# Column parts for the scale weights, five V banks for batch 0, and a new text order in a DiT attention block on one core

## The chip, the cores and the metric

The kernel runs on one core of one Trainium2 chip. The metric is device microseconds of one execution (lower is better), as the median of several runs. The four runs of the kernel before lie 0.3% apart (120.02 to 120.33 us). "Ratio" means throughout: the mean time of one kernel's fast runs over the mean time of the kernel before's fast runs of the same rounds, so it is not quite the ratio of the medians that are quoted beside it. Two runs of experiments were marked slow (over 1.5% above the fastest of their kernel); they are named, and no ratio uses them. The medians in the tables are of all runs.

TensorE is the matmul engine, VectorE and ScalarE do elementwise work, and the DMA engines bring weights from memory. The weight loads are issued in program order by SyncE's queue.

## The reference, cut to what matters

Two streams, image (2 x 256 tokens) and text (2 x 32 tokens), with D = 1152, bf16. Both are layer-normed and modulated by columns of `silu(c) @ wmod` (shift, scale, gate), projected to q, k, v, attend to each other jointly, and are projected out behind the gate.

```python
mod_i = (_silu(c) @ wmod_img).reshape(B, 6, 1, D)   # shift, scale, gate are used
mod_t = (_silu(c) @ wmod_txt).reshape(B, 6, 1, D)
hi = _layernorm(x_img) * (1 + sci) + shi ; ht = _layernorm(x_txt) * (1 + sct) + sht
qkvi = hi @ wqkv_img ; qkvt = ht @ wqkv_txt
# q, k, v = text and image tokens one behind the other
p = softmax(q k^T * D**-0.5) ; a = p v
out_i = x_img + gai * (ai @ wo_img) ; out_t = x_txt + gat * (at @ wo_txt)
```

There are 14 weight matrices of 1152 x 1152 (2.65 MB each), 37 MB in all, and they are read once.

## The kernel before

The kernel keeps five weights at a time in SBUF, the on-chip memory. Each weight goes into one of five slots, and a load into a slot can't be issued before the last reader of that slot's previous weight is done. As all loads stand in one queue, a load that waits also holds up those behind it: in the trace of the change the text gate's load is issued at 80.78 us, and the next one, for the image output weights, starts at 82.42 us.

```python
def load_w(slot, src, c0, splits=(D,)):      # columns c0.. of src into slot "w<slot>"
    ...
w_sc_i = wtile(0)                            # image scale
w_v_i = wtile(1)                             # image V
for b in range(B):
    nc.sync.dma_start(x_i[:, b * TPB:(b + 1) * TPB, :], ...)
SCC = (0, 4, 7, K8, KT)
for r0, r1 in zip(SCC, SCC[1:]):             # scale by groups of 128 rows, whole rows of 2304 bytes
    nc.sync.dma_start(w_sc_i[:, r0:r1, :], sc_v[:, r0:r1, :])
for r0, r1 in ((0, 1), (1, 2), (2, 3), (3, 5), (5, 7), (7, KT)):
    nc.sync.dma_start(w_v_i[:, r0:r1, :], v_v[:, r0:r1, :])
w_sh_i = load_w(2, wmod_img, 0)
w_q_i = load_w(3, wqkv_img, 0)
w_sh_t = load_rows(0, wmod_txt, 0)           # load_rows: three DMAs of three row groups each
w_k_i = load_w(4, wqkv_img, D)
w_sc_t = load_w(1, wmod_txt, D)
w_q_t = load_w(2, wqkv_txt, 0)
w_k_t = load_w(3, wqkv_txt, D)
w_v_t = load_w(1, wqkv_txt, 2 * D)
w_ga_i = load_w(0, wmod_img, 2 * D)          # image gate
w_ga_t = load_w(2, wmod_txt, 2 * D)          # text gate, in the slot of text q
w_o_i = load_rows(3, wo_img, 0)
w_o_t = load_rows(1, wo_txt, 0)
```

At the start the scale columns are computed by TensorE (`sc_ps`), transposed by VectorE, and multiplied into the normalised and transposed x. The V matmuls follow, then image q and k with text work between the blocks, and then:

```python
# in image k, before its last block: qk_txt(0, w_q_t)
qk_txt(1, w_k_t)
...
scores_txt()
scores_img(0)
img_gate()        # 36 matmuls with w_ga_i; then a 0.59 MB broadcast DMA of the result (tile gb)
scores_img(1)
v_txt()
p_transposes(0)
txt_gate()        # 36 matmuls with w_ga_t, row groups 0 to 8 in order
attn_pair(G[0], G[1])
...               # rest of attention, then the output projection
```

All TensorE instructions are pinned to program order, so a wait at `txt_gate` stops everything behind it (in the change TensorE runs nothing from 88.8 to 92.5 us).

## Time and profile before

| | before |
|---|---|
| median of 4 runs | 120.25 us (120.02 to 120.33) |
| span of the profiled run | 118.6 us |
| TensorE busy | 112.1 us, 95% |
| first V matmul / image q starts | 14.76 / 35.03 us |
| text gate's rows start / first output matmul | 87.18 / 95.43 us |
| text gate weight: issued, landed | 73.06 us, 85.7 us |

The chain of work that ended last, in order of time (start, length, what):

```profile
2.12 9.85 DMA t<-in_wmod_img_dram
...
13.83 0.49 DVE scc L217
...
14.76 2.12 PE vps L61 x9
...
87.18 1.22 PE gps L61 x36
88.39 2.16 PE aps L61 x18
...
95.43 19.52 PE ps L61 x144
```

At the start the chain is the scale weights' DMA, then their matmuls, the transpose and the first V matmul. From 14.76 us on it is TensorE alone. Two sets of windows follow, at the start and before the text gate. A row has the window in us, its length, the busy time of TensorE, its weight loads, VectorE, ScalarE and GpSimd, each with the number of instructions, and then the granted clock, the DMA engines' busy share and their GB/s:

```profile
4.00:6.00 2.00, 2.00 (x9) 0.72 (x8) 1.57 (x5) 1.33 (x4) 0.59 (x5) 1.00 0.99 392
6.00:8.00 2.00, 2.00 (x11) 0.81 (x9) 1.02 (x4) 1.94 (x7) 0.46 (x4) 1.00 1.02 393
```

```profile
78.00:80.00 2.00, 2.00 (x22) 1.54 (x17) 1.26 (x3) 0.81 (x2) 0.00 (x0) 1.00 1.04 406
80.00:82.00 2.00, 2.00 (x44) 1.32 (x43) 1.68 (x8) 0.96 (x5) 0.00 (x0) 1.00 1.03 410
```

The line of SyncE's queue that issues the text gate weight (start, time spent, what):

```profile
73.06 0.37 SPq L89 DMA_DIRECT2D t<-in_wmod_txt_dram  x1
```

This DMA landed 12.6 us after its issue, at 85.7 us, because the queue still held other bytes in front of it (at 409 GB/s some 5.2 MB moved in that time, and this weight is 2.65 MB of them). It was wanted at 87.18 us, so the slack is 1.5 us.

### The profile page before, as it was taken

The page shows a single profiled execution, that of the slowest core. Times are in us where ns is not written, and L with a number is a line of the kernel's source. Part 1 is how long each engine was busy: PE and PEld are TensorE (multiplying, and loading weights), DVE is VectorE, ACT ScalarE, POOL GpSimd, SP SyncE. Part 2 cuts the span into 40 slices and gives each one's busy share as a digit, 9 for nine tenths or more (in the row PEclk, how much of TensorE's full clock was granted, in tenths as well). Part 3 has the DMA queues.
Part 4 walks back from the last instruction along what each step waited for, and adds up shares of the span by engine and source line. Part 5 has one row for each costly group of instructions (what it writes and reads, how often), then busy time and mean ns, then how long its engine had stood idle before and what let it go on. Part 6 is the DMA issues. An engine that isn't in the chain of part 4 may idle for free.

```text
span 118.6 us, 2515 instructions
## 1 busy us (share of the span) xinstructions
PE 112.1 (95%) x1051; PEld 64.0 (54%) x1059; DVE 75.3 (63%) x157; ACT 41.8 (35%) x86; POOL 10.3 (9%) x31
## 2 busy tenths in 40 slices
PE   4988899999999999999999999999999999999990
PEld 1335544445674444445444457877876666666660
DVE  2568592063966799999999540048685666666571
ACT  4799620041752524323039233345327620000000
POOL 7110000000000000000000000000409017000000
PEclk9999999999999999999999999999999999999998
DMA  4999999999999999999999999999999996220223
GB/s 104 382 392 399 404 410 406 413 412 411 411 389 384 413 412 410 405 413 411 412 413 412 410 407 413 412 404 412 405 408 411 412 389 219 109 89 16 99 50 100
DMA packets 18613, 40.86 MB, mean 345 GB/s; under 512 B 1019, under 2 KB 1547, under 8 KB 18603
## 3 DMA queue, kind: packets, MB, share of 16 engines
q1 hardware_dynamic: 17728, 39.56, 85.7%
q0 software_dynamic: 480, 0.89, 2.2%
q10 hardware_dynamic: 395, 0.26, 0.7%
q8 instruction: 8, 0.13, 0.4%
q14 instruction: 2, 0.02, 0.0%
HBM read 39.38 MB, written 1.34 MB: 343 GB/s over the span
## 4 chain that ended last, share of the span: by engine, by line
PE 86%; DMA 8%; DVE 2%; SPq 1%; issue 1%; DVEq 0%
PE ps L61 52%; PE vps L61 15%; DMA t<-in_wmod_img_dram 8%; PE gps L61 6%; PE aps L61 6%; PE sps L61 5%; PE sc_ps L61 1%; PE pT_ps L64 1%; SPq L104 1%; DVE tmp L629 1%; DVE o L630 0%; DVE scc L217 0%; SPq L108 0%; PE tpt L64 0%; PE tp L64 0%
## 5 line engine op out<-in xcount | busy, mean ns | idle before, releaser
L61 PE MATMUL ps<-xT_i,t 128*128 128x512 bf16 x157 | 35.6, 380 | 0.3
L61 PEld LDWEIGHTS <-t 128*128 128x128 bf16 x324 | 20.4, 98 | 19.2 <-issue 0.7
L395 DVE SCALAR_TENSOR_TENSOR acc_sh<-t,sTf,acc_sh 128x1152 f32<-128x1152 bf16 x16 | 21.3, 1404 | 0.0
L61 PE MATMUL ps<-t,aT 128*128 128x384 bf16 (+3 forms) x153 | 20.2, 308 | 0.0
L61 PE MATMUL vps<-t,hS_i 128*128 128x512 bf16 (+1 forms) x106 | 17.8, 325 | 0.3 <-DVE hS_i L248 0.2
L61 PEld LDWEIGHTS <-aT 128*128 128x128 bf16 (+1 forms) x153 | 13.0, 101 | 7.1 <-issue 0.5
L61 PEld LDWEIGHTS <-hS_i 128*128 128x128 bf16 x108 | 9.0, 98 | 8.8 <-DVE hS_i L248 0.3
L629 DVE TENSOR_TENSOR tmp<-ps,gb 128x384 bf16<-128x384 f32 (+2 forms) x13 | 6.8, 526 | 6.3 <-PE ps L61 6.3
L346 ACT ACTIVATE qkT<-ps 128x512 bf16<-128x512 f32 (+2 forms) x11 | 6.2, 561 | 12.1 <-PE ps L61 12.1
L61 PE MATMUL wps<-warm 128*128 128x512 bf16 x25 | 7.7, 458 | 1.6 <-DVE unit L132 1.5
L481 POOL DMA_DIRECT2D mod_scratch<-g_sb x4 | 2.5, 634 | 76.6 <-ACT g_sb L174 76.6
L348 ACT CAST qkT<-ps 128x512 bf16<-128x512 f32 (+2 forms) x11 | 5.9, 554 | 8.3 <-PE ps L61 8.3
L172 DVE CAST v_i<-vps 128x512 bf16<-128x512 f32 x5 | 3.5, 692 | 8.2 <-PE vps L61 8.2
L553 DVE TENSOR_TENSOR half<-sps,half 64x288 f32<-64x288 f32 x1 | 0.4, 448 | 9.0 <-ACT half L552 9.0
L587 DVE TENSOR_SCALAR aT<-aps,svc 128x288 bf16<-128x288 f32 x9 | 4.5, 518 | 2.6 <-PE aps L61 2.5
L61 PEld LDWEIGHTS <-sT 128*32 128x32 bf16 x180 | 4.5, 96 | 2.8 <-issue 2.2
L174 ACT CAST v_i<-vps 128x512 bf16<-128x512 f32 x4 | 2.3, 580 | 10.0 <-PE vps L61 10.0
L61 PE MATMUL sps<-qkT 128*128 128x288 bf16 (+1 forms) x54 | 5.6, 288 | 0.0
L61 PEld LDWEIGHTS <-warm 128*128 128x128 bf16 x26 | 2.6, 111 | 5.2 <-issue 2.1
L61 PE MATMUL aps<-pT,v_i 128*128 128x288 bf16 x36 | 5.3, 288 | 0.0
L589 ACT ACTIVATE aT<-aps,svc 128x288 bf16<-128x288 f32 x9 | 4.1, 498 | 3.0 <-PE aps L61 2.9
L61 PE MATMUL gps<-t,sT 128*32 128x288 bf16 x144 | 5.1, 287 | 0.0
(104 smaller groups left out, 108.0 us busy)
## 6 DMA issues: line engine op xcount, KB each, us to landing
t<-in_wqkv_txt_dram SPq DMA_DIRECT2D x3, 2592.0 KB, 16.5
t<-in_wmod_img_dram SPq DMA_DIRECT2D x2, 2592.0 KB, 13.9
t<-in_wqkv_img_dram SPq DMA_DIRECT2D x2, 2592.0 KB, 20.1
t<-in_wmod_txt_dram SPq DMA_DIRECT2D x2, 2592.0 KB, 15.5
t<-in_wmod_txt_dram SPq DMA_DIRECT2D x3, 864.0 KB, 14.7
t<-in_wo_img_dram SPq DMA_DIRECT2D x3, 864.0 KB, 12.3
t<-in_wo_txt_dram SPq DMA_DIRECT2D x3, 864.0 KB, 11.4
t<-in_wqkv_img_dram SPq DMA_DIRECT2D x3, 576.0 KB, 9.2
```

Of the source, the lines that this page charges most:

```text
L61: return pin(nc.tensor.matmul(*a, **k))
L64: return pin(nc.tensor.transpose(*a, **k))
L104: nc.sync.dma_start(x_i[:, b * TPB:(b + 1) * TPB, :], x_img[b].rearrange("(p t) d -> p t d", t=TPB))
L172: nc.vector.tensor_copy(out_ap, in_ap)
L174: nc.scalar.copy(out_ap, in_ap)
L346: nc.scalar.mul(out_ap, in_ap, SCALE)
L348: nc.scalar.copy(out_ap, in_ap)
L395: pin(eng.scalar_tensor_tensor(acc[:, b, :], w[:, kt, :], sTf[:, kt, b:b + 1], acc[:, b, :], op0=ALU.mult, op1=ALU.add))
L481: nc.gpsimd.dma_start(gsc[si, b, :].rearrange("(g j) -> g j", g=NGG), g_sb[b:P:32, :])
L587: nc.vector.tensor_scalar(dst, tiles[(b, dt)][:], bias, None, op0=ALU.add)
L589: nc.scalar.activation(dst, tiles[(b, dt)][:], ACT.Identity, bias=bias)
L629: nc.vector.tensor_mul(tmp[:, 0:n], ps[:, 0:n], gb[:, b, c0:c0 + n])
```

## The change

The early part tries to start V sooner. The scale weights are loaded and used in two column parts (512 and 640 columns, so rows of 1024 and 1280 bytes), x of batch 1 is loaded behind part one and V row 0, and V of batch 0 runs over its first four row groups in five PSUM banks while part two is still on its way. The load of image q is cut into two column parts too. The late part moves text q behind the image gate, loads the image gate ahead of text V, and loads both gates by rows. Cut to its core (`...` marks cuts; the evacuation, transpose and V helpers that serve the early part are left out):

```diff
-    for b in range(B):
+    def load_x(b):
         nc.sync.dma_start(x_i[:, b * TPB:(b + 1) * TPB, :], ...)
...
+    KA = 4
+    SCP = ((0, KA), (KA, KT))
+    load_x(0)
+    load_sc(0, ((0, 4), (4, K8), (K8, KT)))       # 512 columns
+    load_v(((0, 1),))
+    load_x(1)
+    load_v(((1, 2), (2, 3), (3, KA)))
+    load_sc(1, ((0, 5), (5, K8), (K8, KT)))       # 640 columns
+    load_v(((KA, 5), (5, 7), (7, KT)))
...
-    w_q_i = load_w(3, wqkv_img, 0)
+    w_q_i = load_w(3, wqkv_img, 0, (5 * P, D - 5 * P))
...
     w_k_t = load_w(3, wqkv_txt, D)
+    w_ga_i = load_rows(0, wmod_img, 2 * D)
     w_v_t = load_w(1, wqkv_txt, 2 * D)
-    w_ga_i = load_w(0, wmod_img, 2 * D)
-    w_ga_t = load_w(2, wmod_txt, 2 * D)
+    w_ga_t = load_rows(2, wmod_txt, 2 * D)
...
-    A0 = [(0, 0), (1, 0), (0, 1), (1, 1)]
+    A0 = [(0, 0), (1, 0), (0, 1), (1, 1), (0, 2)]
...
-    qk_img(w_k_i, 1, {1: (txt_shift_split, txt_rows_scale,),
-                      6: (txt_rows_shift, txt_cols_shift, txt_modulate),
-                      8: (lambda: qk_txt(0, w_q_t),)})
+    qk_img(w_k_i, 1, {1: (txt_transposes, txt_shift_split), 3: (txt_rows_scale,),
+                      7: (txt_rows_shift, txt_cols_shift, txt_modulate)})
...
-    scores_txt()
     scores_img(0)
     img_gate()
+    qk_txt(0, w_q_t)
+    scores_txt()
     scores_img(1)
```

More of the change, by code (lines that the diff above doesn't have):

```diff
@@ L55, with tr_tile @@
     ps_mm = ctx.enter_context(tc.tile_pool(name="ps_mm", bufs=6, space=PSUM))
-    ps_tr = ctx.enter_context(tc.tile_pool(name="ps_tr", bufs=2, space=PSUM))
+    ps_tr = ctx.enter_context(tc.tile_pool(name="ps_tr", bufs=1, space=PSUM))
+    tr_turn = [0]
+    def tr_tile(shape, dtype, which=None, name="tr"):
+        if which is None:
+            which = tr_turn[0] % 2
+            tr_turn[0] += 1
+        return ps_tr.tile(shape, dtype, tag="tr%d" % which, name=name)
     pin = tc.keep_in_program_order
@@ L102, with load_sc, load_v @@
     sc_v, v_v = wview(wmod_img, D), wview(wqkv_img, 2 * D)
-    for b in range(B):
+    def load_x(b):
         nc.sync.dma_start(x_i[:, b * TPB:(b + 1) * TPB, :], x_img[b].rearrange("(p t) d -> p t d", t=TPB))
-    SCC = (0, 4, 7, K8, KT)
-    for r0, r1 in zip(SCC, SCC[1:]):
-        nc.sync.dma_start(w_sc_i[:, r0:r1, :], sc_v[:, r0:r1, :])
-    for r0, r1 in ((0, 1), (1, 2), (2, 3), (3, 5), (5, 7), (7, KT)):
-        nc.sync.dma_start(w_v_i[:, r0:r1, :], v_v[:, r0:r1, :])
+    KA = 4
+    SCP = ((0, KA), (KA, KT))
+    def load_sc(part, rows):
+        c0, c1 = SCP[part][0] * P, SCP[part][1] * P
+        for r0, r1 in rows:
+            nc.sync.dma_start(w_sc_i[:, r0:r1, c0:c1], sc_v[:, r0:r1, c0:c1])
+    def load_v(rows):
+        for r0, r1 in rows:
+            nc.sync.dma_start(w_v_i[:, r0:r1, :], v_v[:, r0:r1, :])
+    load_x(0)
[5 more added lines that the diff above has]
+    load_v(((KA, 5), (5, 7), (7, KT)))
     w_sh_i = load_w(2, wmod_img, 0)
-    w_q_i = load_w(3, wqkv_img, 0)
+    w_q_i = load_w(3, wqkv_img, 0, (5 * P, D - 5 * P))
     w_sh_t = load_rows(0, wmod_txt, 0)
@@ L157 @@
     pin(nc.vector.tensor_mul(s18[:], c18[:], e18[:]))
-    sT_ps = ps_tr.tile([P, B * KT], bf, tag="tr")
+    sT_ps = tr_tile([P, B * KT], bf)
     tr(sT_ps[:], s18[:], ident[0:B * KT, 0:B * KT])
     sT = const.tile([P, KT, B], bf)
-    warm_up(14)
+    warm_up(10)
     def silu_cols():
@@ L175, in evac, with ln_stats @@
         evac_idx[0] += 1
-    def ln_stats(x_ap, np_, between=None):
+    def ln_stats(x_ap, np_, between=None, at=1):
         stats = small.tile([P, NCH, 6], f32, tag="stats")
         for k in range(NCH):
-            if k == 1 and between:
+            if k == at and between:
                 between()
@@ L185, in ln_stats, with ln_sum @@
         return mv
-    def ln_sums(x_ap, junk):
-        sm = small.tile([P, 3], f32, tag="lnact")
-        pin(nc.scalar.activation(junk, x_ap, ACT.Copy, scale=1.0 / D, accum_out=sm[:, 0:1]))
-        pin(nc.scalar.activation(junk, x_ap, ACT.Square, scale=float(D) ** -0.5, accum_out=sm[:, 1:2]))
-        return sm
+    def ln_sum(x_ap, junk, sm, col):
+        if col == 0:
+            pin(nc.scalar.activation(junk, x_ap, ACT.Copy, scale=1.0 / D, accum_out=sm[:, 0:1]))
+        else:
+            pin(nc.scalar.activation(junk, x_ap, ACT.Square, scale=float(D) ** -0.5, accum_out=sm[:, 1:2]))
     def ln_var(sm):
@@ L218, in mod_cols_of, with sc_rows @@
         return t
-    sc_ps = ps_mm.tile([P, KT, LW], f32, tag="mm")
-    def sc_rows(r0, r1):
+    sc_ps = [ps_mm.tile([P, KA, LW], f32, tag="mm", name="sc_a"), None]
+    sc1_i = const.tile([P, KT, LW], f32, name="scc", tag="scc")
+    def sc_rows(part, r0, r1):
+        c0, c1 = SCP[part]
+        ps = sc_ps[part]
         if r0 == 0:
             for g in range(NGG):
-                mm(sc_ps[LW * g:LW * g + LW].rearrange("p c l -> p (c l)"), lhsT=unit[:], rhs=warm[:, 0:KT * LW],
-                   start=True, stop=False, tile_position=(0, LW * g))
+                mm(ps[LW * g:LW * g + LW].rearrange("p c l -> p (c l)"), lhsT=unit[:],
+                   rhs=warm[:, 0:(c1 - c0) * LW], start=True, stop=False, tile_position=(0, LW * g))
@@ L227, in sc_rows @@
         for kt in range(r0, r1):
             for g in range(NGG):
-                mm(sc_ps[LW * g:LW * g + LW], lhsT=sT32[:, kt, :], rhs=group(w_sc_i, kt, g),
+                mm(ps[LW * g:LW * g + LW], lhsT=sT32[:, kt, :], rhs=group(w_sc_i, kt, g)[:, c0:c1],
                    start=False, stop=(kt == KT - 1), tile_position=(0, LW * g))
-    def x_transposes(k0, b):
-        tr_pool = b == 1 or k0 < 6
-        tp = (ps_tr if tr_pool else ps_mm).tile([P, 3, NI], bf, tag="tr" if tr_pool else "mm", name="tp")
-        for kt in range(k0, k0 + 3):
-            for t in range(TPB):
-                i = b * TPB + t
-                tr(tp[:, kt - k0, t * P:(t + 1) * P], xn_i[:, i, kt * P:(kt + 1) * P], ident[:])
-        dst = xT_i[:, k0:k0 + 3, b * NI:(b + 1) * NI]
-        def copy_out():
-            pin(nc.vector.tensor_copy(dst, tp[:]) if k0 == 3 else nc.scalar.copy(dst, tp[:]))
-        return copy_out
@@ L246, in x_scale, with sc_cols, x_transposes @@
-    def x_scale(k0, k1, b):
+    def sc_cols(part):
+        c0, c1 = SCP[part]
+        pin(nc.vector.transpose(sc1_i[:, c0:c1, :].rearrange("p c l -> p (c l)"),
+                                sc_ps[part][:].rearrange("p c l -> p (c l)")))
+    def x_transposes(k0, k1, tiles, which):
+        n = len(tiles)
+        tp = tr_tile([P, k1 - k0, n * P], bf, which, name="tp")
+        for kt in range(k0, k1):
+            for t, i in enumerate(tiles):
+                tr(tp[:, kt - k0, t * P:(t + 1) * P], xn_i[:, i, kt * P:(kt + 1) * P], ident[:])
+        return lambda op: pin(op(xT_i[:, k0:k1, tiles[0] * P:(tiles[0] + n) * P], tp[:]))
@@ L247, in x_scale @@
+    def x_scale(k0, k1, tiles):
+        b, c0, c1 = tiles[0] // TPB, tiles[0] * P, (tiles[-1] + 1) * P
         for kt in range(k0, k1):
-            pin(nc.vector.tensor_scalar(hS_i[:, kt, b * NI:(b + 1) * NI], xT_i[:, kt, b * NI:(b + 1) * NI],
-                                        sc1_i[:, kt, b:b + 1], None, op0=ALU.mult))
+            pin(nc.vector.tensor_scalar(hS_i[:, kt, c0:c1], xT_i[:, kt, c0:c1], sc1_i[:, kt, b:b + 1], None,
+                                        op0=ALU.mult))
     VW = 512
@@ L253, with v_mm, v_rows, v_keys @@
     accs = {}
-    def v_open(ids, k0, k1, kt_major=True):
-        for key in ids:
-            if key not in accs:
-                accs[key] = ps_mm.tile([P, VW], f32, tag="mm", name="vps")
-        loop = [(kt, key) for kt in range(k0, k1) for key in ids] if kt_major else \
-            [(kt, key) for key in ids for kt in range(k0, k1)]
-        for kt, (i, cc) in loop:
-            mm(accs[(i, cc)][:], lhsT=hS_i[:, kt, i * P:(i + 1) * P], rhs=w_v_i[:, kt, cc * VW:(cc + 1) * VW],
-               start=(kt == 0), stop=(kt == KT - 1), skip_group_check=True)
-            if kt == KT - 1:
-                evac(v_i[:, i, cc * VW:(cc + 1) * VW], accs[(i, cc)][:])
-    A0 = [(0, 0), (1, 0), (0, 1), (1, 1)]
-    A1 = [(2, 0), (3, 0)]
+    def v_mm(kt, key):
+        i, cc = key
+        if key not in accs:
+            accs[key] = ps_mm.tile([P, VW] if cc < 2 else [P, TPB, P], f32, tag="mm", name="vps")
+        acc = accs[key]
+        if cc < 2:
+            mm(acc[:], lhsT=hS_i[:, kt, i * P:(i + 1) * P], rhs=w_v_i[:, kt, cc * VW:(cc + 1) * VW],
+               start=(kt == 0), stop=(kt == KT - 1), skip_group_check=True)
+        else:
+            for t in range(TPB):
+                mm(acc[:, t, :], lhsT=hS_i[:, kt, (i + t) * P:(i + t + 1) * P], rhs=w_v_i[:, kt, 2 * VW:D],
+                   start=(kt == 0 and t == 0), stop=(kt == KT - 1), skip_group_check=True)
+        if kt == KT - 1:
+            if cc < 2:
+                evac(v_i[:, i, cc * VW:(cc + 1) * VW], acc[:])
+            else:
+                evac(v_i[:, i:i + TPB, 2 * VW:D], acc[:])
+    def v_rows(ids, k0, k1):
+        for kt in range(k0, k1):
+            for key in ids:
+                v_mm(kt, key)
+    def v_keys(ids, k0, k1):
+        for key in ids:
+            for kt in range(k0, k1):
+                v_mm(kt, key)
+    A0 = [(0, 0), (1, 0), (0, 1), (1, 1), (0, 2)]
     def ln_norm_dve(i, mv):
@@ L274, in ln_norm_act @@
         ln_norm(x_i[:, i, :], sm[:, 0:1], ln_rstd(sm[:, 2:3], P, sign=-1.0), P, xn_i[:, i, :])
-    s0 = ln_sums(x_i[:, 0, :], xn_i[:, 0, :])
+    V, A = nc.vector.tensor_copy, nc.scalar.copy
+    T0, T2, T3 = (0, 1), (2,), (3,)
+    sm0, sm3 = [small.tile([P, 3], f32, tag="lnact", name="sm") for _ in range(2)]
+    for col in range(2):
+        ln_sum(x_i[:, 0, :], xn_i[:, 0, :], sm0, col)
     m1 = ln_stats(x_i[:, 1, :], P, between=silu_cols)
-    ln_var(s0)
+    ln_var(sm0)
     ln_norm_dve(1, m1)
-    ln_norm_act(0, s0)
@@ L281 @@
-    s2 = ln_sums(x_i[:, 2, :], xn_i[:, 2, :])
-    m3 = ln_stats(x_i[:, 3, :], P)
-    ln_var(s2)
-    r3, r2 = ln_rstd(m3[:, 1:2], P), ln_rstd(s2[:, 2:3], P, sign=-1.0)
-    ln_norm(x_i[:, 3, :], m3[:, 0:1], r3, P, xn_i[:, 3, :])
-    ln_norm(x_i[:, 2, :], s2[:, 0:1], r2, P, xn_i[:, 2, :])
-    for out in [x_transposes(k0, 0) for k0 in (0, 3, 6)]:
-        out()
-    sc_rows(0, 4)
-    warm_up(3)
-    sc_rows(4, 7)
-    warm_up(1)
-    out01 = x_transposes(0, 1)
-    sc_rows(7, K8)
-    sc_rows(K8, KT)
@@ L296 @@
-    out31 = x_transposes(3, 1)
-    sc1_i = mod_cols_of(sc_ps, "scc")
-    out01()
-    x_scale(0, 3, 0)
-    out61 = x_transposes(6, 1)
-    v_open(A0, 0, 3)
-    out31()
-    out61()
-    for k0 in (0, 3, 6):
-        for b in range(B):
-            if k0 or b:
-                x_scale(k0, k0 + 3, b)
-    v_open(A1, 0, 3)
-    v_open(A0 + A1, 3, KT - 2)
-    v_open(A0 + A1, KT - 2, KT, kt_major=False)
+    ln_norm_act(0, sm0)
+    sc_rows(0, 0, 4)
+    warm_up(2)
+    sc_rows(0, 4, K8)
+    out_a = x_transposes(0, 2, T0, 0)
@@ new lines @@
+    sc_rows(0, K8, KT)
+    out_b = x_transposes(2, 5, T0, 1)
+    out_a(A)
+    sc_cols(0)
+    x_scale(0, 2, T0)
+    out_b(V)
+    x_scale(2, KA, T0)
+    v_rows(A0, 0, 1)
+    out_c = x_transposes(5, KT, T0, 0)
+    v_rows(A0, 1, KA)
+    m2 = ln_stats(x_i[:, 2, :], P)
+    for col in range(2):
+        ln_sum(x_i[:, 3, :], xn_i[:, 3, :], sm3, col)
+    ln_norm_dve(2, m2)
+    out_c(A)
+    ln_var(sm3)
+    out_a = x_transposes(0, KA, T2, 1)
+    out_a(A)
+    sc_ps[1] = tr_tile([P, KT - KA, LW], f32, 0, name="sc_b")
@@ new lines @@
+    sc_rows(1, 0, 5)
+    x_scale(0, KA, T2)
+    ln_norm_act(3, sm3)
+    out_b = x_transposes(KA, KT, T2, 1)
+    out_b(A)
+    v_rows([(2, 0)], 0, KA)
+    sc_rows(1, 5, K8)
+    sc_rows(1, K8, KT)
+    sc_cols(1)
+    out_a = x_transposes(0, K8, T3, 1)
+    for kt in range(KA, KT):
+        x_scale(kt, kt + 1, T0)
+        x_scale(kt, kt + 1, T2)
+    out_a(A)
+    v_rows(A0 + [(2, 0)], KA, KA + 1)
+    out_b = x_transposes(K8, KT, T3, 0)
+    out_b(A)
+    v_rows(A0 + [(2, 0)], KA + 1, KT - 2)
@@ L312, in mod_rows_of @@
+    x_scale(0, KT, T3)
+    v_keys(A0 + [(2, 0)], KT - 2, KT)
+    v_keys([(3, 0)], 0, KT)
     def mod_rows_of(w, lhs):
-        gps = ps_tr.tile([P, KT, LW], f32, tag="tr")
+        gps = tr_tile([P, KT, LW], f32)
         for kt in range(KT):
@@ L318, in mod_rows_of @@
         return gps
-    v_open([(2, 1)], 0, KT)
+    v_keys([(2, 1)], 0, KT)
     p_sh = mod_rows_of(w_sh_i, sT32)
@@ L333 @@
     pin(nc.scalar.dma_start(x_t[:], xt_flat[:, :]))
-    v_open([(3, 1)], 0, KT)
-    def v_last():
-        vps = ps_mm.tile([P, NIT, P], f32, tag="mm")
-        for i in range(NIT):
-            for kt in range(KT):
-                mm(vps[:, i, :], lhsT=hS_i[:, kt, i * P:(i + 1) * P], rhs=w_v_i[:, kt, 2 * VW:D],
-                   start=(kt == 0), stop=(kt == KT - 1))
-        evac(v_i[:, :, 2 * VW:D], vps[:])
+    v_keys([(3, 1), (2, 2)], 0, KT)
     def qk_evac(out_ap, in_ap, blk):
@@ L383, in txt_transposes @@
     def txt_transposes():
-        tpt = ps_tr.tile([P, KT, NTT], bf, tag="tr")
+        tpt = tr_tile([P, KT, NTT], bf)
         for kt in range(KT):
@@ L423, in txt_rows_shift @@
     def txt_rows_shift():
-        gps = ps_tr.tile([P, KT, LW], f32, tag="tr")
+        gps = tr_tile([P, KT, LW], f32)
         rows["sh"] = vec_rows(halves[acc_sh.name], gps,
@@ L500, in txt_gate @@
                                     gsc[1, b, :].rearrange("(r g j) -> g r j", r=2, g=2)[g].partition_broadcast(NT))
-    v_last()
     shift_v_rows()
-    qk_img(w_q_i, 0, {1: (txt_ln,), 2: (txt_shift_part(0, 3),), 5: (txt_shift_part(3, 6),),
-                      6: (txt_transposes,), 8: (txt_shift_part(6, KT),)})
-    qk_img(w_k_i, 1, {1: (txt_shift_split, txt_rows_scale,),
-                      6: (txt_rows_shift, txt_cols_shift, txt_modulate),
-                      8: (lambda: qk_txt(0, w_q_t),)})
+    qk_img(w_q_i, 0, {1: (txt_shift_part(0, 3),), 3: (txt_ln,), 4: (txt_shift_part(3, 6),),
+                      7: (txt_shift_part(6, KT),)})
+    qk_img(w_k_i, 1, {1: (txt_transposes, txt_shift_split), 3: (txt_rows_scale,),
+                      7: (txt_rows_shift, txt_cols_shift, txt_modulate)})
     qk_txt(1, w_k_t)
@@ L558, in p_transposes @@
     def p_transposes(b):
-        pT_ps = ps_tr.tile([P, 3, NTOK], bf, tag="tr")
+        pT_ps = tr_tile([P, 3, NTOK], bf)
         for qi in range(TPB):
```

## The prediction

> **What bounds the kernel now.** The chain of waits is TensorE for 86%, and DMA only at the start. The timeline shows TensorE without a gap from the first V matmul (14.76 us) to the last output matmul (about 115 us): the windows give 99.9 us busy in those 100.2 us. Until 14.76 it waits for the scale weights: x (1.18 MB) and scale (2.65 MB) must land (first four rows at 9.85 us, next three at 12.0, the last about 13), then a 0.48 us column transpose and a 0.28 us scaling. The DMA engines are almost as tight: 405 to 413 GB/s, busy share 1.04, from 4 us to 95 us. Each 2.65 MB weight costs 6.5 us of it, and weights land about 1.5 us after the transferred bytes reach their place in the order.
>
> **What the change does at the start.** Part one needs only 0.59 MB of x and 1.18 MB of scale, landing at about 8.5 us (my estimate from the landing curve); the layernorm of batch 0 already ended at 8.8 us. So V of batch 0 can start near 10 us. Rows 0 to 3 in five banks cost 4 x (4 x 0.216 + 2 x 0.056) = 3.9 us, and tile 2 another 0.86 us, all in time that was warm-up. Then TensorE waits again: scale part two is byte 5.0 MB and V row 4 byte 5.3 MB of the order, so the second scaling comes at about 17.4 us (17 to 18). From there V is dense. Sum: 4.8 us done early, 2.6 us later dense start: gain about 2.1 us (1.5 to 2.7) when q starts (35.0 becomes about 32.9). [...]
>
> **What happens to that gain.** The bytes are unchanged, so the text gate weight stays at byte 33.0 MB; it landed at 73.06 + 12.6 = 85.7 us and was needed at 87.18: slack 1.5 us. TensorE 2.1 us earlier meets that. Worse, it lies in the slot of text q. Text q moves behind the image gate, so the slot comes free at about 78.5 us instead of 73.06, when the bytes before it (30.4 MB) have passed at about 78: the queue runs dry for about 1.3 us. Worse again, the image gate comes 5 us earlier, so its broadcast (0.59 MB, 1.4 us of bandwidth, which today runs at 89 to 96 us) now shares the engines with the text gate weight. Estimated landing 87 to 88.5 us against 85 us wanted: TensorE waits 1.5 to 3 us before the text gate's rows (loading by rows hides only the first two thirds), and attention starts at 87 to 88.8 us against 88.4 now. After it all is TensorE work as before (26.6 us).
>
> So most of the early gain is given back. Floor: without stall the text gate still can't end before 86.1 us, a gain of 2.3 us.
>
> **Predicted:** 119.7 us, 118.3 to 121.0. Faster by over 2%: 9%; within 2%: 85%; slower: 6%.
>
> **To check:** first V matmul near 10 us; TensorE gap near 15 to 17.5 us ending on scale or V weights; q starting at 32.3 to 33.5; a DMA wait of over 1 us at the text gate's rows; a dip in GB/s near 78 to 80 us; attention to end unchanged.
>
> **What would make it wrong:** the text shift's VectorE sums (22.9 us) end later and stop the key blocks; scale part two lands later than the curve says; the broadcast does not collide or the queue does not run dry (then 118.2).

The sum of the early gain: 3.9 + 0.86 = 4.76 us done early, less 17.4 - 14.76 = 2.64 us of later dense start, is 2.12 us, about 2.1. With about 1.5 us lost at the text gate, 120.25 - 2.1 + 1.5 comes to the 119.7 us.

For its other terms the traces show: 90 matmuls of 128x512 in 19.53 us (0.217 us each, the chain of the change from 34.92 us on), and in the trace of before six of 128x128 in 0.33 us (0.055 each), 407 GB/s on average from 4 to 95 us with slices down to 382, and 33.07 MB through the weight queue by 84.2 us, 1.5 us before the text gate weight landed.

## More of the kernel before

Lines of the profile's page. The rows cut the span into 40 slices of 2.97 us; a digit is the busy share in tenths, PEclk is the granted TensorE clock in tenths, GB/s is what the DMA engines moved.

```profile
PE   4988899999999999999999999999999999999990
...
PEclk9999999999999999999999999999999999999998
...
GB/s 104 382 392 399 404 410 406 413 412 411 411 389 384 413 412 410 405 413 411 412 413 412 410 407 413 412 404 412 405 408 411 412 389 219 109 89 16 99 50 100
```

TensorE is full from the sixth slice on, at full clock, and the DMA engines are full too: 382 to 413 GB/s in slices 2 to 33, over 400 in 26 of these 32.

## The result, and the profile after

| | before | after |
|---|---|---|
| median | 120.25 us (4 runs) | 126.53 us (126.27 to 127.74, 4 runs) |
| ratio of fast runs | | 1.0545, 95% interval 1.0475 to 1.0616 |
| span of the profiled run | 118.6 us | 125.8 us |
| mean granted clock, profiled run | 0.995 | 0.973 (the other three runs: 0.986, 0.969, 0.986) |
| first V matmul / dense V stretch | 14.76 / 14.76 us | 10.62 / 19.37 us |
| image q starts | 35.03 us | 34.92 us |
| text gate's rows start | 87.18 us | 87.02 us |
| first output matmul | 95.43 us | 102.59 us |

The change is slower, well outside the stated range. The profiled run of the change was the slowest of its four (127.74 us), so the sums below are somewhat larger than those of the median. The same lines of the page (slices of 3.15 us here):

```profile
PE   5998979999999999999999999998159999999990
...
PEclk9999999999999999999999999999955899999999
...
GB/s 130 295 363 402 397 403 412 413 397 384 402 374 410 408 409 412 411 412 413 415 379 396 397 411 405 98 294 358 339 404 413 378 410 223 101 0 94 94 47 94
```

Three things are new: a hole in the GB/s row (98, slice 26) with three weak slices behind it, a hole in TensorE (slices 29 and 30), and a granted clock of 5 tenths from the end of that hole on. The chain:

```profile
8.46 9.44 DMA t<-in_wmod_img_dram
...
17.94 0.39 PE sc_b L68 x12
...
19.37 1.36 PE vps L68 x7
...
34.92 19.53 PE ps L68 x90
...
81.89 10.59 DMA t<-in_wmod_txt_dram
...
92.53 0.91 PE gps L68 x9
...
102.59 19.52 PE ps L68 x144
```

The chain's last wait at the start now ends with part two of the scale weights, at 17.94 us. Between 19.37 us and the text gate the chain is TensorE as before, and q starts only 0.11 us sooner. Then 10.59 us of DMA, a last third of the text gate's weight, stand in the chain, and the first output matmul comes at 102.59 instead of 95.43 us. The early windows and those around the text gate:

```profile
4.00:6.00 2.00, 2.00 (x7) 0.56 (x6) 1.59 (x5) 1.57 (x4) 0.51 (x4) 1.00 0.93 272
6.00:8.00 2.00, 2.00 (x13) 0.75 (x15) 1.28 (x4) 1.84 (x6) 0.54 (x4) 1.00 1.03 321
```

```profile
78.00:80.00 2.00, 2.00 (x73) 1.79 (x62) 1.10 (x5) 0.26 (x2) 0.33 (x1) 1.00 0.64 248
80.00:82.00 2.00, 2.00 (x48) 1.37 (x45) 0.00 (x0) 1.18 (x3) 1.05 (x2) 1.00 0.30 46
82.00:84.00 2.00, 2.00 (x20) 1.43 (x20) 1.48 (x5) 0.92 (x4) 0.89 (x2) 1.00 0.84 264
...
88.00:90.00 2.00, 0.55 (x12) 0.33 (x12) 0.73 (x2) 0.00 (x0) 0.00 (x0) 1.00 0.93 305
90.00:92.00 2.00, 0.00 (x0) 0.00 (x0) 0.00 (x0) 0.00 (x0) 0.00 (x0) 0.91 1.03 400
92.00:94.00 2.00, 1.47 (x15) 0.75 (x15) 0.00 (x0) 0.40 (x1) 0.00 (x0) 0.50 1.03 399
```

Read the last three columns of the second fence. The DMA engines moved 248, 46 and 264 GB/s from 78 to 84 us, where before they moved over 400. At 88 to 90 us they are weak again (305). TensorE has no work from 88.8 to 92.5 us, and the granted clock is 0.50 in the window from 92 to 94 us. Finer windows show where it changes: it falls at 91.6 us and is back at 98.5 us, 6.8 us later. The issue of the text gate weight, and the matmuls that wait for it:

```profile
80.78 1.59 SPq L104 DMA_DIRECT2D t<-in_wmod_txt_dram  x3
```

```profile
87.02 0.55 PE L68 MATMUL gps<-t,sT 128*32 128x288 bf16 x12
88.27 0.55 PE L68 MATMUL gps<-t,sT 128*32 128x288 bf16 x12 [0.70 <-DMA t<-in_wmod_txt_dram]
92.53 0.91 PE L68 MATMUL gps<-t,sT 128*32 128x288 bf16 x12 [3.71 <-DMA t<-in_wmod_txt_dram]
93.37 1.62 PE L68 MATMUL aps<-pT,v_i 128*128 128x288 bf16 x6
```

The slot comes free when text q is done, at 80.7 us instead of 73.0, so the load is issued at 80.78. TensorE does the first third of the rows, waits 0.70 us for the second and 3.71 us for the last. After that, matmuls of the same form take 1.8 times as long: the six `aps<-pT,v_i` at 93.37 us take 1.62 us, the same six 0.91 us in the trace of before:

```profile
88.32 0.91 PE L61 MATMUL aps<-pT,v_i 128*128 128x288 bf16 x6
```

The loss to the first output matmul is 7.16 us in the profiled runs. The waits are 4.41 us of it. From the start of the last third to the first output matmul it takes 102.59 - 92.53 = 10.06 us, where before the same work took 0.41 us (a third of the gate's 1.22) + 7.04 us (95.43 - 88.39) = 7.45 us. That is 2.6 us more, lost to the half clock. The rest, about 0.1 us, is the small start advantage against the ends of the split matmul groups.

### The profile page after: what moved, and what is told of

Read it like the earlier page. It is cut to its first block, busy times and chain, and to the rows that moved or that the text cites. A ratio compares the mean times of both kernels' runs of the same rounds, so it can differ in the third digit from the quotient of the medians.

```text
span 125.8 us, 2609 instructions
## 1 busy us (share of the span) xinstructions
PE 115.4 (92%) x1093; PEld 64.9 (52%) x1093; DVE 76.0 (60%) x166; ACT 43.9 (35%) x89; POOL 10.3 (8%) x31
## 4 chain that ended last, share of the span: by engine, by line
PE 73%; DMA 21%; SPq 1%; DVE 1%; issue 0%
PE ps L68 48%; DMA t<-in_wmod_img_dram 13%; PE vps L68 10%; DMA t<-in_wmod_txt_dram 8%; PE aps L68 7%; PE tr L68 3%; PE sps L68 2%; PE gps L68 2%; PE tr L71 1%; SPq L104 1%; PE sc_b L68 1%; DVE tmp L680 1%; DVE o L681 0%; SPq L120 0%; SPq L112 0%
## 5 line engine op out<-in xcount | busy, mean ns | idle before, releaser
L68 PE MATMUL vps<-t,hS_i 128*128 128x512 bf16 (+1 forms) x108 | 18.5, 326 | 0.6 <-DVE hS_i L273 0.6
L533 POOL DMA_DIRECT2D mod_scratch<-g_sb x4 | 2.5, 634 | 83.1 <-DVE g_sb L194 73.1
L68 PEld LDWEIGHTS <-sT 128*32 128x32 bf16 x216 | 5.0, 97 | 8.0 <-issue 7.4
L68 PE MATMUL wps<-warm 128*128 128x512 bf16 x20 | 7.1, 513 | 1.5 <-DVE unit L154 1.5
L68 PE MATMUL gps<-t,sT 128*32 128x288 bf16 x72 | 3.3, 313 | 4.4 <-DMA t<-in_wmod_txt_dram 4.4
L68 PE MATMUL aps<-pT,v_i 128*128 128x288 bf16 x36 | 6.8, 344 | 0.0
L273 DVE TENSOR_SCALAR hS_i<-xT_i,scc 128x128 bf16<-128x128 bf16 (+1 forms) x27 | 5.1, 258 | 1.5 <-ACT xT_i L268 1.3
L268 ACT COPY xT_i<-tp 128x512 bf16<-128x512 bf16 (+3 forms) x6 | 4.1, 689 | 5.0 <-PE tp L71 4.9
L194 DVE CAST v_i<-vps 128x512 bf16<-128x512 f32 (+1 forms) x5 | 3.1, 636 | 3.4 <-PE vps L68 3.4
L68 PE MATMUL ps<-hT_t,t 128*128 128x64 bf16 x162 | 5.1, 193 | 0.0
```

Of the source, the lines that this page charges most:

```text
L68: return pin(nc.tensor.matmul(*a, **k))
L194: nc.vector.tensor_copy(out_ap, in_ap)
L268: return lambda op: pin(op(xT_i[:, k0:k1, tiles[0] * P:(tiles[0] + n) * P], tp[:]))
L273: pin(nc.vector.tensor_scalar(hS_i[:, kt, c0:c1], xT_i[:, kt, c0:c1], sc1_i[:, kt, b:b + 1], None, op0=ALU.mult))
L533: nc.gpsimd.dma_start(gsc[si, b, :].rearrange("(g j) -> g j", g=NGG), g_sb[b:P:32, :])
```

## The experiments

My theory after the traces: the early part gains nothing because its short loads arrive late, and the whole loss comes from the late part: the text gate weight shares a slot with text q, so the DMA queue runs dry, the image gate's broadcast then takes bandwidth from the late weight, TensorE waits, and in the wait its granted clock falls (to 0.50, at 91.6 us). Rivals: the early part itself does harm; the broadcast alone is the cause; the slow matmuls have another cause. Each run is compared with the kernel before on the same chip. All gave correct results. Numbers 1 to 4, then 5, 6, 8, 9, then 10 and 11 ran together.

| run | what | median us | before us | ratio (95%) |
|---|---|---|---|---|
| change | | 126.53 | 120.25 | 1.0545 (1.0475 to 1.0616) |
| e1 | change, text gate in another slot | 120.41 | 120.44 | 0.9987 (0.9965 to 1.0010) |
| e2 | change, broadcast later | 124.07 | 120.44 | 1.0309 (1.0267 to 1.0351) |
| e3 | change, 16 dummy matmuls before the last third | 125.46 | 120.44 | 1.0395 (1.0352 to 1.0437) |
| e4 | early part alone | 121.21 | 120.44 | 1.0053 (1.0030 to 1.0076) |
| e5 | late part alone | 127.74 | 120.20 | 1.0611 (1.0554 to 1.0668) |
| e6 | before, scale loads cut in columns | 121.48 | 120.20 | 1.0100 (1.0074 to 1.0127) |
| e8 | change, 3 + 9 dummies | 127.87 | 120.20 | 1.0561 (1.0468 to 1.0654) |
| e9 | e1 with a 640-column part one | 120.27 | 120.20 | 1.0002 (0.9976 to 1.0029) |
| e10 | change, 20 dummies ahead of all thirds | 125.91 | 120.37 | 1.0453 (1.0424 to 1.0482) |
| e11 | whole rows, x of batch 1 behind | 120.87 | 120.37 | 1.0028 (1.0006 to 1.0050) |

### e1: another slot for the text gate weight

```diff
-    w_ga_t = load_rows(2, wmod_txt, 2 * D)
+    w_ga_t = load_rows(4, wmod_txt, 2 * D)
```

Slot 4 holds image k, which is done before text k starts.

> The change with one edit: the text gate weight goes into the slot of image k (free at about 72.3 us) instead of text q (free at about 80.7 us). Theory 1 (slot wait, then a cooled TensorE): the DMA queue no longer runs dry near 80 us, the weight lands at 87 to 89 us instead of 92.5, TensorE waits at most 1.5 us at the gate's rows, the granted clock stays at 1.0, and the time falls from 126.4 to 119.8 to 121.5 us. Rival (the collision with the image gate's broadcast is the main delay): the queue stays full, but the wait stays over 2.5 us and the time over 123 us. Rival (the early part or the new order itself is slow): the time stays above 124 us.

Measured: 120.41 us, ratio 0.9987. The load is issued at 72.37 us. Windows and chain of e1:

```profile
78.00:80.00 2.00, 2.00 (x73) 1.94 (x68) 1.04 (x4) 0.26 (x3) 0.49 (x1) 1.00 1.04 407
80.00:82.00 2.00, 2.00 (x45) 1.33 (x42) 0.09 (x1) 1.06 (x3) 0.89 (x2) 1.00 1.04 409
...
92.00:94.00 2.00, 2.00 (x21) 1.25 (x19) 1.40 (x3) 1.49 (x3) 0.00 (x0) 1.00 1.05 408
```

```profile
86.93 1.22 PE gps L68 x36
...
95.22 19.52 PE ps L68 x144
```

No hole in the DMA rate, no wait of TensorE for this weight, clock 1.00 in these windows, and the first output matmul at 95.22 us, 0.21 us before that of the kernel before. One digit removes the whole loss; the theory had even left room for a wait of up to 1.5 us. The rivals that blamed the early part or the new order as such fall: both are still in e1. So is the broadcast, but it was issued at 85.6 us here instead of 83.1, and by the time it moved (0.43 MB from 89 to 91 us, two packets from 85 to 87) the text gate weight had landed, whose rows start at 86.93 us without a wait; e1 alone does not acquit it, so e2 moves it by itself.

### e2: the broadcast after the text gate's matmuls

```diff
     def img_gate():
         mod_rows(w_ga_i, 0)
-        for b in range(B):
-            nc.gpsimd.dma_start(gb[:, b, :], gsc[0, b, :].partition_broadcast(P))
...
     def txt_gate():
         mod_rows(w_ga_t, 1)
+        img_gate_bcast()       # the two DMAs of above, now pinned to program order
```

> The change, with the image gate's broadcast issued after the text gate's matmuls instead of before. Theory 1: the broadcast's 0.59 MB took about 2 us of the engines at the text gate weight's expense; without it the last third lands at 90 to 91 us instead of 92.5, the wait for it is about 2 us instead of 3.7, the clock perhaps stays up, and the time is 122 to 125 us. Rival (broadcast harmless): the landing stays within 0.5 us of 92.5 and the time within 0.7 us of 126.4.

Measured: 124.07 us, ratio 1.0309. The last third could start at 89.44 us instead of 92.53. The load was issued 0.7 us sooner in this run (80.04 us), so 2.4 us of the 3.1 are the broadcast's:

```profile
89.44 0.55 PE L68 MATMUL gps<-t,sT 128*32 128x288 bf16 x12 [1.55 <-DMA t<-in_wmod_txt_dram]
```

The two waits are 2.1 us in all instead of 4.4, and the clock stayed at 1.00 in the profiled run (of the other three, one had a mean of 0.986, and it was the slowest, 124.93 us). A new wait of 1.3 us for the image output weights appeared behind it. So the collision is real and is worth about 2.4 us of landing time, but the hole in the DMA rate (109 and 9 GB/s at 79 to 81 us) is still there, and without e1's edit the kernel stays 3% slow. The broadcast makes the slot wait worse; it is not the root.

### e4 and e5: each part alone

e4 keeps the early part, with the text order, gate order and gate loads of before. e5 is the kernel before with those of the change. The edits are the two halves of the diff above.

> The early part of the change alone: column parts, load order, five V banks, split q load; the text order, gate order and gate loads of before. Theory: the early part is worth about 0.1 us by itself in the profile (q starts at 34.9 against 35.0 us), so the time is 119.8 to 120.6 us. Rival (the early part itself makes later waits or slow matmuls): over 121.5 us.

> The kernel before with only the late part of the change: its text order, its gate order and its gate loads by rows. Theory: the late part alone makes the whole loss: q starts at 35.0 us as before, the text gate weight is issued only near 80.7 us, lands near 92 us, TensorE waits about 4 us and then runs about 2.6 us slower at half clock; time 125.5 to 127 us. Rival (the loss needs both parts): below 123 us.

Measured: e4 121.21 us, ratio 1.0053, in the gap between what the two theories of it expected; e5 127.74 us, ratio 1.0611, a little above its range. The late part makes the whole loss by itself: in e5 the DMA rate falls to 58 GB/s at 78 to 80 us, TensorE waits 2.57 and 1.67 us at the text gate, and the granted clock is 0.50 from 91.3 to 98.1 us:

```profile
90.09 0.55 PE L61 MATMUL gps<-t,sT 128*32 128x288 bf16 x12 [2.57 <-DMA t<-in_wmod_txt_dram]
92.31 0.91 PE L61 MATMUL gps<-t,sT 128*32 128x288 bf16 x12 [1.67 <-DMA t<-in_wmod_txt_dram]
```

The early part alone is not neutral: it costs 0.5%. Its loads run about a microsecond behind those of before (in the change, with the same early part, 5.0 MB had passed at 15.8 us instead of 14.9, an estimate from the windows), and the text scale weight comes too late for the rows that the old order puts into image k's second block:

```profile
55.15 1.29 PE L68 MATMUL tr<-t,sT 128*32 128x288 bf16 x36 [0.81 <-DMA t<-in_wmod_txt_dram]
```

With the new text order, which asks for that weight two blocks later, e1 has no such wait. So the new order does answer a need that the early part makes; only the slot of the text gate spoils it.

### e6 and e9: what the column parts cost the loads

e6 is the kernel before with each scale load cut into its two column parts, computation unchanged:

```diff
-        nc.sync.dma_start(w_sc_i[:, r0:r1, :], sc_v[:, r0:r1, :])
+        for c0, c1 in ((0, 512), (512, D)):
+            nc.sync.dma_start(w_sc_i[:, r0:r1, c0:c1], sc_v[:, r0:r1, c0:c1])
```

> The kernel before with each load of the scale weights cut into its two column parts of 1024 and 1280 bytes per row, same bytes, same order of rows, same computation. Theory: the short packets cost: about 55 ns each, whether 1024 or 1280 bytes, so the rate falls to about 300 to 370 GB/s while they run, the first V matmul moves from 14.8 to 15.4 to 16.0 us and the time rises by 0.5 to 1.2 us. Rival (packet size harmless, as my prediction had it): first V matmul within 0.25 us of 14.76, time within 0.3 us.

The 55 ns come from the trace of the change: from 4 to 6 us 547 packets took 93.3% of 16 engines' time, 54.6 ns each (rows of 1024 bytes), from 12 to 14 us 608 took 105.9%, 55.7 ns each (mostly rows of 1280 bytes).

Measured: 121.48 us, ratio 1.0100; the first V matmul starts at 15.55 us instead of 14.76. Windows of e6, to set beside those of before:

```profile
4.00:6.00 2.00, 2.00 (x8) 0.65 (x7) 1.44 (x5) 1.29 (x3) 0.46 (x4) 1.00 1.00 363
6.00:8.00 2.00, 2.00 (x11) 0.88 (x9) 1.02 (x4) 1.93 (x7) 0.60 (x5) 1.00 1.03 358
```

The same bytes in shorter rows move at 363 and 358 GB/s instead of 392 and 393. So part of the late arrival comes from cutting the rows. In the change, though, part one alone is on its way at 4 to 8 us and moves at only 272 and 321 GB/s. e9 asked whether longer rows cure that, with e1's slot and part one of 640 columns (`KA = 5`):

> The slot edit, and part one of the scale weights 640 columns wide instead of 512: part one now has 1280 byte rows, which moved at about 395 GB/s in the trace, and one more V row runs before the second part. Theory (short rows made the early loads late): part one lands no later than 8.9 us in spite of 25% more bytes, the dense V stretch is about one row (1.2 us) shorter, q starts at 33.6 to 34.4 us and the time is 119.2 to 120.0 us. Rival: no better than 120.4 us.

Measured: 120.27 us, ratio 1.0002; q starts at 34.53 us. The theory missed. Windows of e9:

```profile
4.00:6.00 2.00, 2.00 (x9) 0.67 (x8) 1.63 (x5) 1.55 (x4) 0.55 (x4) 1.00 0.94 293
6.00:8.00 2.00, 2.00 (x28) 0.91 (x27) 1.23 (x4) 1.86 (x6) 0.51 (x4) 1.00 0.96 310
...
14.00:16.00 2.00, 2.00 (x14) 1.02 (x13) 0.71 (x2) 1.51 (x5) 0.00 (x0) 1.00 1.08 384
```

Rows of 1280 bytes move at 293 and 310 GB/s at 4 to 8 us, hardly better than 1024, though rows of the same size moved at 395 GB/s in the change at 12 to 16 us (part two of the scale weights). The last line shows the same for rows of 1024 bytes: e9's part two, rows of 1024 bytes, moves at 384 GB/s from 14 to 16 us, where the change's part one, in rows of the same length, got 272 and 321. So it is neither a fixed time per row, as I had assumed in both expectations, nor the row length alone: narrow loads were slow early in the run and nearly at full rate later. In time per packet: the rows of 1024 bytes took 54.6 ns at 4 to 6 us in the change and 45.0 ns at 14 to 16 us in e9 (772 packets, 108.5% of 16 engines' time). Why a narrow part one is slow just there stays open.

### e3, e8 and e10: keeping the clock up

These put dummy matmuls on TensorE into the waits, to separate the wait from what it does to the clock. e3: 16 before the last third. e8: 3 before the second third, 9 before the last. e10: 20 ahead of all thirds.

```diff
         gps = ps_mm.tile([P, VC], f32, tag="mm")
+        if si == 1:                                   # e10
+            wps2 = ps_mm.tile([P, 512], f32, tag="mm", name="wps2")
+            for _ in range(20):
+                mm(wps2[:], lhsT=warm[:, 0:P], rhs=warm[:], start=True, stop=True)
         for kt in range(KT):
```

> The change, with 16 dummy matmuls (about 3.5 us) in the wait before the last third of the text gate's rows. Theory: the wait costs twice, once as time and once as half clock afterwards (2.6 us). The landing stays at about 92.5 us, the clock stays at 1.0 after it, and the time is 123.3 to 124.3 us. Rival (the slow matmuls after the wait have another cause, or the dummy work comes on top): the time stays at 126 us or more.

> The change with 3 dummy matmuls before the second and 9 before the last third of the text gate's rows, 2.6 us in all, shorter than the 4.4 us of waits, so that they end before the weights land (in the run with 16 they ended about a microsecond too late). Theory: waits as in the change, clock 1.0 throughout, attention from the gate's last third to the first output matmul in about 7.5 us instead of 10.1; time 123.2 to 124.6 us. Rival: at 126 us or above.

> The change with 20 dummy matmuls (4.3 us) ahead of all three thirds of the text gate's rows, so that no wait before or between the thirds can reach the length after which the clock fell (in the run with 12 dummies the wait before the second third was 3.4 us and the clock fell there). Theory: the last third still lands near 92.2 us, the clock stays at 1.0, the stretch from the last third to the first output matmul is 7.5 us instead of 10.1, the time is 123.8 to 125 us. Rival (half clock costs nothing of its own): 126 us or more.

Measured: e3 125.46 us (one of its four runs, 129.59, was slow), e8 127.87 us (one slow run, 129.06), e10 125.91 us. None reached its expected time; without the slow run e3's median is 125.10 us. In e3 the second third came at 89.06 us, later than in the change, and the dummies behind it ended 0.5 us after the last third was there (it landed at about 92.7 us, 10.8 us after its issue, and was used at 93.17 us). Its clock stayed at 1.00 through these windows, and from the last third to the first output matmul (100.69 us) it took 7.52 us. In e8 the wait came before the second third instead:

```profile
91.12 0.91 PE L68 MATMUL gps<-t,sT 128*32 128x288 bf16 x12 [3.38 <-DMA t<-in_wmod_txt_dram]
91.96 3.13 PE L68 MATMUL wps<-warm 128*128 128x512 bf16 x9
```

It waited 3.38 us there, the clock fell before the dummies began, and nine of them took 3.13 us at half clock, on the critical path. e8 thus tells nothing about the cost of the clock, except that a wait of 3.38 us was enough to lose it here. e10 is the clean one:

```profile
86.42 4.49 PE L68 MATMUL wps<-warm 128*128 128x512 bf16 x19
90.84 0.92 PE L68 MATMUL gps<-t,sT 128*32 128x288 bf16 x24
92.69 0.55 PE L68 MATMUL gps<-t,sT 128*32 128x288 bf16 x12 [0.94 <-DMA t<-in_wmod_txt_dram]
```

The last third starts at 92.69 us, as in the change, the mean granted clock of the run is 1.0, and from there to the first output matmul (100.29 us) it takes 7.60 us, not 10.06. That confirms, with e3's 7.52 us, the half clock as a loss of its own of 2.5 us in the profiled runs. Over all runs it is less. From the change to e3 the ratio falls from 1.0545 to 1.0395, about 1.8 us, and the intervals lie apart (this is for e3's three fast runs, which kept the clock; the run left out as slow had 0.987); to e10 it falls to 1.0453, about 1.1 us, but there the intervals still overlap (1.0475 to 1.0616 and 1.0424 to 1.0482). The granted clocks say why. At half clock for t us, a run of 125.8 us has a mean clock of 1 - t/2/125.8, so 0.973 stands for about 6.8 us, and 0.986, which two of the change's four runs had, for about 3.5 us. The traces have both lengths: the clock was at half for 6.8 us in the change and in e5, and for 3.4 us in e8 (90.6 to 94.1 us).

### e11: the attempt at a better version

Scale weights in whole rows and one part, x of batch 1 behind V row 2, five banks for batch 0, q in one load, text gate in slot 4.

```diff
+    load_x(0)
+    load_sc(0, ((0, 4), (4, 7), (7, K8), (K8, KT)))      # whole rows
+    load_v(((0, 1), (1, 2), (2, 3)))
+    load_x(1)
+    load_v(((3, 4), (4, 5), (5, 7), (7, KT)))
...                      # the transposes of batch 1 between V rows 4 and 6
```

> An attempt at a version that keeps the idea of the change and leaves out what the runs found costly: scale weights in whole rows and in one part, x of batch 1 loaded behind V row 2, five V banks for batch 0, q load in one piece, text gate weight in the slot of image k. Theory: the last scale row lands about 1.4 us earlier than before because 0.59 MB of x stand behind it, the first V matmul comes at 12.7 to 13.6 us instead of 14.8, the transposes of batch 1 (1 us) move into the V stretch, q starts at 33.8 to 34.4 us and the time is 119.0 to 119.8 us. Rival (V rows or x of batch 1 now arrive too late): waits of over 0.7 us inside the V stretch and no gain.

Measured: 120.87 us, ratio 1.0028. The first V matmul started at 13.12 us, as hoped, but q at 34.81 us: of the 1.6 us, 1.2 us came back as the transposes of batch 1 (0.62 + 0.56 us in the chain), which before had filled the time in which TensorE waited for the scale weights, and most of the rest in waits and small gaps. No version beats the kernel before by more than its interval; e1 and e9 equal it.

## Why the prediction was wrong, point by point

Three steps failed: the early gain of 2.1 us (0.11 came), the wait of 1.5 to 3 us (4.41 came), and the work after it, taken as unchanged (2.6 us more came, at half clock).

- **What bounds the kernel: right.** TensorE without a gap after 14.76 us, DMA near full, slack of 1.5 us at the text gate.
- **"gain about 2.1 us ... when q starts": wrong, 0.11 us.** The dense V stretch began at 19.37 us, not 17.4. Two thirds of this are loads that came late: by 10 us the change had moved 2.71 MB where the kernel before had moved 3.04 (the GB/s of the windows times their length), and the last rows of part two were waited for until 17.94 and 18.34 us, not 16.6 (17.4 less 0.8 us for transpose and scaling). The other third is the step from those rows to the first V matmul, which took 1.4 us instead of 0.8. The term that failed is the landing of the narrow loads, and with it the small allowance for their rows (cut above), which no run had measured. Early in the run they cost this: e6 measured 7 to 9% lower rates and a first V matmul 0.8 us later for scale weights in both parts; part one alone moved 18 to 31% slower than the loads of before in the same windows (272 and 321 against 392 and 393 GB/s). Later in the run the difference was smaller: e9's rows of 1024 bytes moved at 384 GB/s from 14 to 16 us, 7% below the 412 of before. From the windows I estimate that 5.0 MB had passed at 15.8 us instead of 14.9. That is 0.9 of the 1.3 us by which the rows were late; the other 0.4 us is not traced.
- **The wait at the text gate: right in its mechanism, too small in its terms.** I named the slot, the dry queue and the broadcast, in that order, and said "TensorE waits 1.5 to 3 us". It waited 4.41 us. "the slot comes free at about 78.5 us" became 80.7, because the 2.1 us of early gain were not there. "the queue runs dry for about 1.3 us" became about 3.2 us of lost transfer: from 78 to 83 us the engines moved 0.72 MB where 410 GB/s would have moved 2.05 (an estimate from the windows), and the rate was back at 394 GB/s only at 83 us, 2.2 us after the issue. The broadcast took more than the 1.4 us that I gave its 0.59 MB: without it, e2's last third landed 2.4 us sooner, counted from the issue. In the 2 us from 87 us both queues moved, the broadcast's 69 packets with 61% of the engines' time and the weights' 101 packets with 30%.
- **"After it all is TensorE work as before (26.6 us)": wrong.** I did not think of the clock. The clock was at half for 6.8 us in the change and in e5 and for 3.4 us in e8. In the change it fell at 91.6 us, 2.8 us after TensorE's last matmul had ended (88.82 us), in e8 2.9 us after it, and in e5 only 0.6 us after a third of the rows that had run between waits of 2.57 and 1.67 us. What sets these times was not shown. It cost 2.5 us in the profiled runs and on average 1.8 us by e3, 1.1 us by e10 (not clear of noise).
- **"So most of the early gain is given back": the sum.** I had -2.1 and about +1.5 us. What came was -0.1, +4.4 for the wait and up to +2.6 for the clock. The range of 118.3 to 121.0 us rested on the early gain paying for the wait, and it counted the wait's price only once.
- **"slower: 6%": too low.** A slack of 1.5 us had been spent by a slot that comes free 7.7 us later, and what stood against it was one estimate.

## What to carry to other kernels

When a change moves the last use of a buffer, look at once at what is loaded into that buffer next, and count from the new release: issue, a slow restart of a dry queue (2.2 us from the issue to 394 GB/s in the change), the bytes, and whatever else now runs beside them. A TensorE wait can cost more than its length: in the change the waits of 4.41 us were followed by 2.6 us more at half clock. In the profiled runs here a single wait of 2.14 us (e3) kept the clock, and waits of 3.38 (e8) and 3.71 us (the change) lost it; so did two waits of 2.57 and 1.67 us with 0.55 us of work between them (e5), so a little work in between need not save it. An early start bought with narrower loads must be paid from the rate that those narrower loads really get (here 272 and 321 GB/s instead of 392 and 393), which has to be measured at the point of the run where they stand.

## What the runs measured and leave open

- A narrow load early in the run moved 18 to 31% slower (272 and 321 against 392 and 393 GB/s), and rows of 1280 bytes 293 and 310 GB/s there but 395 GB/s later in the run, rows of 1024 bytes 384 GB/s (e9, 14 to 16 us, 7% below the kernel before). What makes the difference between early and late, the runs do not tell.
- After the dry queue the load was issued at 80.78 us, its first bytes moved at about 81.8 us, 1.0 us after the start of the issue; the engines moved 46 GB/s in the window from 81 to 82 us and 134 in the next, and reached 394 GB/s only in the one from 83 us.
- The image gate's broadcast is two DMAs of 288 KB, each read from a row of 2.2 KB. From 87 to 89 us in the change its queue moved 69 packets and 0.29 MB for 61% of 16 engines' time, 283 ns each (0.61 x 16 x 2 us / 69); in the kernel before, from 93 to 95 us, 133 packets and 0.50 MB took 149 ns each. Why it was slower in the change stays open.
- The clock fell 2.8 us (change), 2.9 us (e8) and 0.6 us (e5) after the last matmul and stayed at half for 6.8, 3.4 and 6.8 us. What sets these lengths stays open.
